# Moving the router's logits of the last two token tiles out of TensorE's tail, with their sums made ahead

## The chip, the cores and the metric

The kernel runs on one core of one Trainium2 chip. The metric is the device time of one execution in microseconds (us); the kernel before has a median of 738.65 over three runs. A core has five engines that run side by side, each with its own queue of instructions: TensorE (PE, matrix products), VectorE (DVE), ScalarE (ACT), GpSimd (POOL) and SyncE (SP, which here issues nearly all transfers). An engine takes its instructions in the order of its queue; one that waits holds up all that stand behind it.

## What is computed

The reference has three stages. Retention attention (2 x 8 heads, 768 positions, head width 64, blocks of 64) gives x of 1536 tokens x 512. A dense mixture of four experts follows, weighted by each token's domain probabilities, and then a mixture of eight experts of which each token takes the one with the greatest logit:

```python
# first mixture, dense
p = domain_probs / (domain_probs.sum(-1, keepdims=True) + 1e-09)
for e in range(4):
    h = np.maximum(x @ w1[e], 0.0)            # 512 -> 1024
    out += p[:, e:e + 1] * (h @ w2[e])        # 1024 -> 512
# second mixture, x is now the first one's output
logits = x @ w_gate                           # 512 -> 8
expert_idx = np.argmax(logits, axis=1)
...
for e in range(8):                            # only the tokens of expert e
    h = np.maximum(x[mask] @ w1[e], 0.0)
    out[mask] = gate_w[mask, None] * (h @ w2[e])
```

All is float32. TensorE takes float32r here, so each operand is split into a high and a low part and each product is three (high x high, high x low, low x high); `mm3` at L595 is that product.

## The kernel before

The 1536 tokens are 12 tiles of 128. After the attention the first mixture runs in 16 units k = 0 to 15, each of them half an expert (512 hidden features) for half of the tokens (six tiles): k = 0 to 7 do the first half, 8 to 15 the second. Units 1 to 13 are fast units (`fast_unit`): the first products (L740, tiles named b) are made by seven products of half-size blocks instead of eight, written into PSUM banks, copied by ScalarE (L747, tiles u), summed by VectorE (`total`, L754, also on tiles u) and split into ht_..h and ht_..l (L602, L603); then six second products y (L595), each added into acc by VectorE (L636). The seven products share a few PSUM banks: the last product of a unit goes into two banks that `total` has read just before. In units 1 to 6 VectorE also makes the next units' first weights in the combined forms that the products need (L182, L251) and SP stores them in DRAM (kept, L247) for the second half. Work that isn't the products' own is hung on hooks: `hook1(i)`, i = 0 to 13, stands behind the 14 half products of a fast unit, and `hook2(j)`, j = 0 to 5, behind its second products.

The sum of the blocks that a fast unit needs comes from `x_sum` (L703), which for the second half's tokens runs in units 2 to 5, one call each at i = 1. x2 holds the second half's attention output, 128 x 4 x 768 float32, from the attention on until unit 7 makes its splits; from then on its place serves as a ring of five pieces of 512 columns in which rows of the router's weights lie, one row on all partitions.

The router's logits of six tiles are sums by VectorE, `logit_v` (L846): the product of a tile of acc (128 x 512) with one router row, reduced to one column of lg_v; 48 of them run in units 8 to 12. Units 14 and 15 run together as three blocks of 256 tokens (768, 1024, 1280, named by the first token), with plain products h and y; each block's steps are also hung on hooks, numbered through all the blocks. The choice of a tile (`route_choose`: maximum mx, score sc, m_all, one-hot oh, df, seen; L889 to L907) and its rank (`route_rank`, products with a triangle and with ones, L918, L920) are placed by `route_at` at such hooks.

The last block's two tiles are y (tile 10) and z (tile 11). y's second products are plain; z's are made in two halves of 256 columns (`last_dense`, tile yz, added to acc at L658). Their logits come from TensorE: acc is transposed (`route_x`, tile rtr, L858), copied, and multiplied with the router's weights (`route_lg`, tile lg, L869). Then come choice, rank, the selection (`first_sel`, sel), and the products that place the two tiles' rows among those of the second mixture's first expert (`first_place`, L1037, into px, where the rows that were gathered from DRAM have been transposed by `first_T`, L1006). VectorE and ScalarE split px into xg (L1418, L1419), and the first expert's products g (L1479, L1480) begin.

At the start, 54 matmuls on ones (`warmup`, L1098) run before the first scores; SP loads the attention's data meanwhile.

Of the kernel before, what the change touches and what calls it, by code (L numbers as in the profile page):

```python
# [77 lines left out]
def body(ctx: ExitStack, tc: tile.TileContext, lam, att, dp, w1a, w2a, wg, wgt, w1b, w2b, out):  # L78
# [29 lines left out]
    lg_v = const.tile([P, VT, E2], F32, name="lg_v")  # L108
# [33 lines left out]
    wt = {}  # L142
    raws = [rawp]
# [40 lines left out]
    def split_plain(n, c, only=""):  # L184
        b = blocks[n]
        k = b[1]
        if c == 0 and only != "l":
            wt[b] = tuple(
                wp.tile([P, 4, HF], F32R, tag=f"w{b[0]}{x}", name=f"w{b[0]}{x}_{b[1]}")
                for x in "hl"  # L190
            )
        if b in EARLY_AT and c < EARLY:
# [24 lines left out]

    kept = {
# [234 lines left out]
    def att_a(c):  # L453
# [7 lines left out]
        for r in range(2):  # L461
            V.tensor_tensor(out=a[r], in0=qk[r], in1=w[:, r], op=ALU.mult)
# [179 lines left out]
    def last_parts(hs, j, c, i):  # L642
        return [
            ((hh[:, j * P:j * P + P], hl[:, j * P:j * P + P]),
             tuple(w[:, f % FC, c] for w in wt[1, KL - 1 + f // FC]))
# [3 lines left out]
    def last_dense(hs, t0, j, m, i):  # L649
        t = t0 // P + j  # L650
        c = slice(m * HD, m * HD + HD)
        if i == 0:
            rt["yz"] = ps_mm.tile([P, 512], F32, tag="mm", name=f"yz{m}")[:, :HD]
        ps = rt["yz"]
# [133 lines left out]
    def open_routing():  # L788
        op = ctx.enter_context(pool("order", 1, side="right"))
        for name, n, d in (  # L790
            ("places", EN, F32), ("caps", EN, F32), ("count", E2, F32), ("place", EN, F32),
            ("cap_e", E2, F32), ("nth", EN, I32), ("tmp", E2 * max(OMAX, E2), F32),
# [41 lines left out]

    def logit_piece(e):
        i = e % RING * DM
        return x2.rearrange("p d t -> p (d t)")[:, i:i + DM]
# [7 lines left out]
    def logit_v(t, e):  # L845
# [4 lines left out]
        if t == TT - 1:  # L850
            logit_load(e + RING)

# [22 lines left out]
    def route_choose(t):  # L875
        rp = rt["rs"]
        if t < VT:
# [79 lines left out]

    def last_sends():
        rp = rt["rs"]
        n = 2  # L960
        two = slice(NC - n, NC)
        sums, far, at_row = (
            rp.tile([P, n], F32, name=f"two{i}", bufs=1) for i in range(3)
        )
        pos = rp.tile([P, n], I32, name="twopos", bufs=1)
        for i in range(n):
            t = NC - n + i
            oh, _, df, _ = rt.pop((t, "chosen"))
            ex = rp.tile([P, E2], F32, tag="ex", name=f"ex{t}")
            A.activation(out=ex, in_=df, func=AF.Exp, accum_out=sums[:, i:i + 1])  # L970
            jk = rp.tile([P, E2], F32, tag="jk", name=f"jk{t}")
# [5 lines left out]
            out=at_row, in0=m2_all[:, two], scalar1=-float(MOST), scalar2=float(E2 * MOST),  # L977
            op0=ALU.mult, op1=ALU.add,
        )
        V.tensor_scalar(  # L980
# [3 lines left out]
        V.tensor_tensor(out=at_row, in0=at_row, in1=far, op=ALU.add)  # L984
        V.tensor_tensor(out=pos, in0=at_row, in1=rk_all[:, two], op=ALU.add)
        V.tensor_scalar(out=sums, in0=sums, scalar1=1e-9, scalar2=None, op0=ALU.add)
        V.reciprocal(acc[:, two, DM], sums)
        for i in range(n):
            t = NC - n + i
            scatter(bins, pos[:, i:i + 1], acc[:, t, :], E2 * MOST, "bins")  # L990
# [10 lines left out]
    def first_T(s):  # L1001
        if s == 0:
            px = [ps_mm.tile([P, 512], F32, tag="mm", name=f"px{d}") for d in range(2)]
            rt["px"] = [px[d // 2][:, d % 2 * CAP:d % 2 * CAP + CAP] for d in range(KD)]
        for d in range(KD):
            T.matmul(  # L1006
                rt["px"][d][:, s * ST:s * ST + ST], rt["xe"][:ST, s, d * P:d * P + P],
                ident[:ST, :ST], start=s == 0 and d % 2 == 0, stop=False, is_transpose=True,
# [34 lines left out]
    def route_order():  # L1043
        count, place, places = od["count"], od["place"], od["places"]
        by_pair = od["tmp"][:, :EN * EN].rearrange("p (a b) -> p a b", a=EN)
        sm = rt["warm"][:, :E2]
# [53 lines left out]
    def keep_up(n):  # L1100
        rt["warm"] = small("warm_rt")
        warmup(rt["warm"], n)


    with tc.manual_schedule():
# [13 lines left out]
        warmup(warm, 54)  # L1119
# [166 lines left out]
        for i, now in enumerate((  # L1286
# [7 lines left out]
            if now[-1] in ((b, 7), (c, 2)):  # L1294
                for d in range(E2 - RING):
                    at(8 + i, logit_load, d if now[-1] == (b, 7) else RING + d)
        route_at(a, 17, 18)
# [7 lines left out]
        for k in FAST:  # L1305
            def logit(n):
                for _ in range(n):
                    if logits:
                        logit_v(*logits.pop(0))
# [12 lines left out]

            def hook2(j):
# [10 lines left out]
                if k in KEPT:  # L1334
                    logit(2 if k == KS else 2 - j % 2)
# [5 lines left out]
            if k == KS - 1:  # L1341
                for e in range(RING):
                    logit_load(e)
                logits = [(t, e) for e in range(E2) for t in range(TT)]
# [5 lines left out]
        for t0 in range(TS, N, 256):  # L1350
# [16 lines left out]
            if last:  # L1367
                split_to(0, K1 + 1, 4)
                state["owed"] = 0
                split_to(1, K1, EARLY)  # L1370
                first_load()
            for j in range(256 // P - last):
                moe1_mm2(KL, hs, t0, j)
                if not last:
                    unit(2 * FC + j)
        assert not plan
        y, z = NC - 2, NC - 1
        low, high = range(KD // 2), range(KD // 2, KD)
        first_parts(y)
        last_dense(hs, t0, 1, 0, 0)  # L1380
        route_x(y)
        last_dense(hs, t0, 1, 0, 1)
        last_dense(hs, t0, 1, 1, 0)
        first_parts(z, slice(0, HD))
        route_x(z, low)
        last_dense(hs, t0, 1, 1, 1)
        route_lg(y)
# [478 lines left out]
```

## Time and profile before

| what | us |
|---|---|
| median of three runs | 738.65 |
| lowest and highest of them | 738.19, 739.57 |
| the profiled execution, its own time | 739.93 |
| its span in the trace | 738.1 |
| attention and unit 0 | 0 to 78.67 |
| fast units 1 to 13, 31.55 each but for the first and the last | 78.67 to 489.88 |
| units 14 and 15 in blocks of 256 tokens | 489.88 to 554.4 |
| last tiles' routing | 554.4 to 568.8 |
| second mixture | 568.8 to 729.84 |
| last sums and stores | to 738.1 |

One profiled execution is read: when each instruction began and how long it took, what it waited for, and what the transfers did. The span is the stretch from its first to its last instruction; 1.8 us of the execution's own time lie around it. The stages are read off the chain of waits, the chain of work that ended last, followed back from the last instruction.

### The profile page before, as it was taken

The page shows a single profiled execution, that of the slowest core. Times are in us where ns is not written, and L with a number is a line of the kernel's source. Part 1 is how long each engine was busy: PE and PEld are TensorE (multiplying, and loading weights), DVE is VectorE, ACT ScalarE, POOL GpSimd, SP SyncE. Part 2 cuts the span into 40 slices and gives each one's busy share as a digit, 9 for nine tenths or more (in the row PEclk, how much of TensorE's full clock was granted, in tenths as well). Part 3 has the DMA queues.
Part 4 walks back from the last instruction along what each step waited for, and adds up shares of the span by engine and source line. Part 5 has one row for each costly group of instructions (what it writes and reads, how often), then busy time and mean ns, then how long its engine had stood idle before and what let it go on. Part 6 is the DMA issues. An engine that isn't in the chain of part 4 may idle for free.

```text
span 738.1 us, 12981 instructions
## 1 busy us (share of the span) xinstructions
PE 727.1 (99%) x4951; PEld 658.9 (89%) x4951; DVE 510.9 (69%) x1140; ACT 313.7 (42%) x690; POOL 81.2 (11%) x86
## 2 busy tenths in 40 slices
PE   9999999999999999999999999999999999999995
PEld 8888989889898988989889898988898998998994
DVE  7557776776756766657677667774696867675883
ACT  4333725243342535424223141541153757565772
POOL 3474000000000000000000002100021013121013
PEclk9999999999999999999999999999999999999998
DMA  8763794626446175455161543361143968765661
GB/s 315 286 217 104 249 262 175 256 93 255 158 180 256 58 284 229 155 202 212 59 257 38 218 156 145 100 200 39 52 113 133 323 222 270 255 209 187 229 231 32
DMA packets 39420, 136.79 MB, mean 185 GB/s; under 512 B 6913, under 2 KB 6913, under 8 KB 34747
## 3 DMA queue, kind: packets, MB, share of 16 engines
q1 hardware_dynamic: 37243, 129.63, 50.6%
q0 software_dynamic: 2112, 6.31, 2.2%
q8 instruction: 40, 0.66, 0.4%
q14 instruction: 25, 0.20, 0.1%
HBM read 102.85 MB, written 33.26 MB: 184 GB/s over the span
## 4 chain that ended last, share of the span: by engine, by line
PE 96%; DVE 1%; ACT 1%; issue 1%; POOL 0%; POOLq 0%; DVEq 0%
PE y L595 36%; PE b L740 26%; PE h L595 7%; PE g L595 5%; PE z L595 3%; PE z L1479 3%; PE g L1479 2%; PE zr L1588 2%; PE qk L395 1%; PE z L1480 1%; PE g L1480 1%; PE xo L529 1%; PE zr L1559 1%; PE warm L1098 1%; PE yz L595 1%; PE gr L595 1%
## 5 line engine op out<-in xcount | busy, mean ns | idle before, releaser
L210 DVE TENSOR_TENSOR w1l<-raw,w1h 128x512 fp32r<-128x512 f32 x124 | 82.4, 688 | 28.5 <-ACT w1h L208 28.1
L636 DVE SCALAR_TENSOR_TENSOR acc<-y,p_sb,acc 128x512 f32<-128x512 f32 x77 | 57.8, 751 | 61.2 <-PE y L595 54.2
L747 ACT COPY u<-b 128x384 f32<-128x384 f32 x78 | 36.4, 479 | 108.6 <-PE b L740 107.1
L208 ACT CAST w1h<-raw 128x512 fp32r<-128x512 f32 x124 | 73.1, 619 | 1.1 <-DMA raw<-in_w2a 1.1
L125 POOL DMA_INDIRECT bins<-acc,pos x10 | 11.2, 1117 | 456.9 <-DVE mx L889 378.5
L740 PE MATMUL b<-xh,w0h 128*128 128x384 f32 x208 | 57.8, 339 | 0.0
L210 DVE TENSOR_TENSOR w0l<-raw,w0h 128x512 fp32r<-128x512 f32 x76 | 51.2, 722 | 0.8 <-ACT w0h L208 0.6
L846 DVE CUSTOM_DVE_ANT_0 x<-acc,x 128x512 f32<-128x512 f32 x72 | 49.4, 687 | 1.0
L208 ACT CAST w0h<-raw 128x512 fp32r<-128x512 f32 x76 | 42.9, 623 | 4.5 <-DMA raw<-in_w1a 4.0
L125 POOL DMA_INDIRECT out<-y,xb x16 | 30.0, 1878 | 132.6 <-DVE y L1625 82.8
L754 DVE TENSOR_TENSOR u<-b,u 128x384 f32<-128x384 f32 x78 | 43.1, 552 | 1.4 <-PE b L740 1.4
L740 PEld LDWEIGHTS b<-xh,w0h 128*128 128x128 f32 x208 | 38.2, 188 | 0.6
L595 PE MATMUL g<-xg,w0h 128*128 128x288 f32 (+1 forms) x192 | 38.1, 294 | 0.0
L595 PE MATMUL h<-xh,w0h 128*128 128x256 f32 x144 | 36.0, 292 | 0.2 <-ACT xh L181 0.2
L740 PE MATMUL b<-xl,w0h 128*128 128x384 f32 x104 | 35.2, 339 | 0.0
L595 PE MATMUL h<-xh,w0l 128*128 128x256 f32 x144 | 34.7, 282 | 0.1
L740 PE MATMUL b<-t1h,w0h 128*128 128x384 f32 x104 | 30.8, 337 | 0.0
L595 PEld LDWEIGHTS g<-xg,w0h 128*128 128x128 f32 x192 | 30.8, 188 | 0.0
L740 PE MATMUL b<-xh,w0l 128*128 128x384 f32 x104 | 28.8, 338 | 0.0
L740 PE MATMUL b<-t4h,w0l 128*128 128x384 f32 x104 | 28.8, 337 | 0.0
L740 PE MATMUL b<-t2h,w0l 128*128 128x384 f32 x104 | 28.7, 337 | 0.0
L740 PE MATMUL b<-t3h,w0h 128*128 128x384 f32 x104 | 28.6, 336 | 0.0
(371 smaller groups left out, 2053.6 us busy)
## 6 DMA issues: line engine op xcount, KB each, us to landing
raw<-in_w2a SPq DMA_DIRECT2D x32, 512.0 KB, 3.5
raw<-in_w1b SPq DMA_DIRECT2D x32, 512.0 KB, 5.7
raw<-in_w2b SPq DMA_DIRECT2D x32, 512.0 KB, 4.4
kept<-w0h SPq DMA_DIRECT2D x12, 1024.0 KB, 7.9
w0h<-kept SPq DMA_DIRECT2D x12, 1024.0 KB, 9.5
raw<-in_w1a SPq DMA_DIRECT2D x18, 512.0 KB, 3.7
att<-in_att SPq DMA_DIRECT2D x12, 512.0 KB, 4.7
kept<-w0l SPq DMA_DIRECT2D x6, 1024.0 KB, 6.6
```

The source lines that it names most:

```text
L125: i = G.indirect_dma_start(out=dst, out_offset=bass.IndirectOffsetOnAxis(ap=idx, axis=0), in_=src, in_offset=None, bounds_check=rows - 1, ...
L208: A.copy(out=hi, in_=t)
L210: V.tensor_tensor(out=lo, in0=t, in1=hi.bitcast(F32), op=ALU.subtract)
L595: T.matmul(ps, l, r, start=first and i == 0, stop=last and i == len(ops) - 1)
L636: V.scalar_tensor_tensor(out=acc[:, t, 0:DM], in0=ps, scalar=p_sb[:, t, e:e + 1], in1=acc[:, t, 0:DM], op0=ALU.mult, op1=ALU.add,)
L740: T.matmul(ps, l[:, d, c], r[:, d, :], start=first and i == 0, stop=i == len(ops) - 1, skip_group_check=not first,)
L747: A.copy(out=t, in_=bank[2, s])
L754: V.tensor_tensor(out=t, in0=bank[b, s], in1=t, op=ALU.add)
L846: V.tensor_tensor_reduce(out=x2.rearrange("p d t -> p (d t)")[:, RING * DM:], in0=acc[:, t, 0:DM], in1=logit_piece(e), scale=1.0, scalar=0 ...
L1479: T.matmul(ps[:, :2 * n], wh, both, start=i == 0, stop=False)
L1480: T.matmul(ps[:, :n], wl, hi, start=False, stop=i == len(parts) - 1)
L1588: T.matmul(ps[s][:st], l[:, c], r, start=h == 0 and j == 0, stop=h == 1 and j == len(ops) - 1)
```

## The change

For the last two tiles the logits no longer come from transposes and products with the router. A logit of a tile is the sum of what the tile has in acc so far, times a router column, and of what the last expert half still adds; the latter is h times (w2 times the router column). So:

- Before the end, VectorE makes the two tiles' logits from their sums so far: 16 more `logit_v`, hung on hooks 1, 3, 5, 6 and 7 of the blocks, where hook 7 has six, and on hooks 15, 16 and 17.
- The second weights of the last expert get eight more columns, w2 times w_gate: the weight tiles of w2 are 520 columns wide, and the right halves of the two tiles' last products are 264 wide. Their last eight columns are added to lg_v, times the expert's probability (`lg_v<-yz`, 128 x 8).
- The eight columns for the last expert's eight row blocks are 64 sums of 512 products over a piece of w2 (`wg_v`, a VectorE product with reduction as in `logit_v`). 40 are hung on units 2 to 6, eight each (hook1 at i = 5, 9, 13 and hook2 at j = 0 to 4), and 24 on units 8 to 12 between the 48 logits. Each piece of w2 (128 x 512, 256 KB) is a load of its own, as is each router row.
- For the first 40, router rows and pieces of w2 lie in x2's place. So x2 is stored to DRAM at the end of unit 1 (`parked<-x`) and read back in unit 7; the four `x_sum` calls of the second half move from units 2 to 5 to unit 1 (i = 3, 5, 9, 11).
- The tail is written in another order: y's right half first, its choice, its left half, z's right half in two parts, z's left half, with the ranks between them; the transposes into px come behind, one bank for each of the four blocks d, in the order 2, 3, 0, 1; part of the places of the last two tiles goes to GpSimd.
- The warm-up has 46 matmuls instead of 54, and the first two attention tiles' product with the decay is made in halves. The loads of two raw pieces and the gathered rows change places at the start of the second mixture.

The diff, cut:

```diff
     def last_dense(hs, t0, j, m, i):
         t = t0 // P + j
-        c = slice(m * HD, m * HD + HD)
+        c = slice(m * HD, m * HD + HD + m * E2)
...
-        if i == 1:
+        if i == 1 and m:
             e = half(KL) // 2
             V.scalar_tensor_tensor(
-                out=acc[:, t, c], in0=ps, scalar=p_sb[:, t, e:e + 1], in1=acc[:, t, c],
-                op0=ALU.mult, op1=ALU.add,
-            )
+                out=lg_v[:, t, :], in0=ps[:, HD:], scalar=p_sb[:, t, e:e + 1],
+                in1=lg_v[:, t, :], op0=ALU.mult, op1=ALU.add,
+            )
...
+    def wg_v(u, e):
+        i = (u % (2 * FC)) * E2 + e
+        V.tensor_tensor_reduce(
+            out=x2_piece(RING), in0=od["wg", u],
+            in1=logit_piece(e) if u >= WG_PIECES - 2 * FC else x2_piece(e % 3), scale=1.0,
+            scalar=0.0, op0=ALU.mult, op1=ALU.add, accum_out=od["lw"][:, i:i + 1],
+        )
...
+        for hook, *now in (
+            (1, (y, 3)), (3, (z, 3)), (5, (y, 4)), (6, (z, 4)),
+            (7, (y, 5), (z, 5), (y, 6), (z, 6), (y, 7), (z, 7)),
+            (15, (y, 0)), (16, (z, 0)), (17, (y, 1), (z, 1), (y, 2), (z, 2)),
+        ):
+            for x in now:
+                at(hook, logit_v, *x)
+        at(12, wg_columns)
...
-                elif KS < k < K1 - 4:
-                    logit(i < 6)
-                elif i == 1 and 1 < k < 6:
-                    x_sum((3, 1, 2, 4)[k - 2], 1)
+                elif 1 < k < KS - 1:
+                    logit(i in (5, 9, 13))
+                elif k in KEPT:
+                    logit(i in (3, 7, 9, 13) and (i > 3 or k > KS))
...
+                if k == 1 and i in (3, 5, 9, 11):
+                    x_sum({3: 3, 5: 1, 9: 2, 11: 4}[i], 1)
+                if k == KS - 1 and i == 0:
+                    SP.dma_start(out=x2, in_=parked)
...
+            if k == 1:
+                SP.dma_start(out=parked, in_=x2)
+                for e in WG_PASSES[0]:
+                    wg_row(e)
+                wg_load(0)
+                wg_load(1)
+                logits = wg_steps(0) + wg_steps(1)
...
-        warmup(warm, 54)
+        warmup(warm, 46)
```

Where the instructions stand. SP, from the last stores of unit 1 to the first loads of unit 2 (kept is the store of the combined weights, raw a piece of weights, x the place of x2), before:

```order
L247 DMA kept_88<-w0h_2_1664 128x2048
L247 DMA kept_88<-w0l_3_1684 128x1024
L167 DMA raw_1753<-in_w2a 128x1024
L167 DMA raw_1794<-in_w2a 128x1024
L247 DMA kept_89<-w0h_0_1889 128x2048
```

and now:

```order
L251 DMA kept_89<-w0h_2_1666 128x2048
L251 DMA kept_89<-w0l_3_1686 128x1024
L1427 DMA parked<-x_103 128x3072
L885 DMA x_103<-in_wgt 128x512 x3
L881 DMA x_103<-in_w2a 128x512 x2
L168 DMA raw_1760<-in_w2a 128x1024
L168 DMA raw_1802<-in_w2a 128x1024
```

Six transfers stand between the last kept store and the next raw pieces; the five loads write the place that the store of x2 reads.

VectorE, in the first products of unit 2 (w1l is the low part of a second weight, u the total of a product, ht its split), before:

```order
L754 TENSOR_TENSOR u_2_1736<-b_2_1773,u_2_1736 128x384
L603 SCALAR_TENSOR_TENSOR ht_001l<-u_2_1736,ht_001h 128x384
L210 TENSOR_TENSOR w1l_1726<-raw_1522,w1h_1725 128x512
L754 TENSOR_TENSOR u_2_1802<-b_2_1785,u_2_1802 128x384
L603 SCALAR_TENSOR_TENSOR ht_110l<-u_2_1802,ht_110h 128x384
```

and now (the rows with lw are a sum and the reading of its result):

```order
L769 TENSOR_TENSOR u_2_1744<-b_2_1780,u_2_1744 128x384
L610 SCALAR_TENSOR_TENSOR ht_001l<-u_2_1744,ht_001h 128x384
L889 ISA x_103,lw<-x_103 128x512
L889 ISA lw 128x1
L213 TENSOR_TENSOR w1l_1734<-raw_1522,w1h_1733 128x512
L769 TENSOR_TENSOR u_2_1810<-b_2_1793,u_2_1810 128x384
L610 SCALAR_TENSOR_TENSOR ht_110l<-u_2_1810,ht_110h 128x384
```

The first sum stands between two splits and ahead of the total u that frees a bank for the last product of the unit.

VectorE in the tail, from the weight splits to y's choice (yz are the last products, lg the logits), before:

```order
L1021 TENSOR_TENSOR al_5877<-acc,ah_5876 128x512
L658 SCALAR_TENSOR_TENSOR acc<-yz_5880,p_sb,acc 128x256
L1021 TENSOR_TENSOR al_5927<-acc,ah_5926 128x256
L658 SCALAR_TENSOR_TENSOR acc<-yz_5913,p_sb,acc 128x256
L889 TENSOR_REDUCE mx_5963<-lg_5948 128x1
L891 SCALAR_TENSOR_TENSOR sc_5965<-lg_5948,mx_5963,desc 128x8
```

and now:

```order
L213 TENSOR_TENSOR wel_1_5959<-raw_5864,weh_1_5958 128x512
L665 SCALAR_TENSOR_TENSOR lg_v<-yz_5971,p_sb,lg_v 128x8
L951 TENSOR_REDUCE mx_5997<-lg_v 128x1
L953 SCALAR_TENSOR_TENSOR sc_5999<-lg_v,mx_5997,desc 128x8
L956 TENSOR_REDUCE m_all<-sc_5999 128x1
L957 TENSOR_SCALAR oh_6001<-sc_5999,m_all 128x8
L963 TENSOR_SCALAR df_5998<-lg_v,mx_5997 128x8
```

y's choice stood behind the sums and low parts of both tiles, and stands now right behind the last weight split.

## Rows read from the trace of the kernel before

**Rows 1.** The page, parts 1 and 4: busy us and share; the chain's shares

```profile
PE 727.1 (99%) x4951; PEld 658.9 (89%) x4951; DVE 510.9 (69%) x1140; ACT 313.7 (42%) x690; POOL 81.2 (11%) x86
...
PE 96%; DVE 1%; ACT 1%; issue 1%; POOL 0%; POOLq 0%; DVEq 0%
```

**Rows 2.** The chain of waits: start us, us, what

```profile
0.99 5.75 PE warm L1098 x54
6.73 1.99 PE qk L395 x32
...
554.42 1.43 PE yz L595 x12
...
568.39 0.43 PE g L1479
```

**Rows 3.** Timeline of SP: start us, us, engine line op out<-in xcount

```profile
1.17 0.89 SPq L340 DMA_DIRECT2D att<-in_att  x2
```

**Rows 4.** Transfers by kind, KB each, median us from issue to landing

```profile
att<-in_att SPq DMA_DIRECT2D x12, 512.0 KB, 4.7
...
x<-in_wgt SPq DMA_DIRECT2D x14, 256.0 KB, 3.2
```

**Rows 5.** Timeline of VectorE in unit 2

```profile
113.21 0.95 DVE L703 TENSOR_TENSOR acc<-x 128x768 f32<-128x768 f32 x1
...
119.89 0.55 DVE L754 TENSOR_TENSOR u<-b,u 128x384 f32<-128x384 f32 x1
...
121.51 0.55 DVE L754 TENSOR_TENSOR u<-b,u 128x384 f32<-128x384 f32 x1
```

**Rows 6.** Windows, units 1, 2: PE, PEld, DVE, ACT, POOL; clock, DMA, GB/s

```profile
78.67:110.42 31.75, 31.75 (x158) 28.16 (x157) 24.34 (x40) 14.80 (x30) 0.53 (x1) 1.00 0.96 293
110.42:141.97 31.55, 31.55 (x157) 28.24 (x157) 21.96 (x36) 12.62 (x25) 0.00 (x0) 1.00 0.56 210
```

**Rows 7.** Timeline of SP: kept stores of units 1, 2; five loads

```profile
106.81 0.33 SPq L247 DMA_DIRECT2D kept<-w0l  x1
...
138.36 0.44 SPq L247 DMA_DIRECT2D kept<-w0l  x1
...
301.38 2.23 SPq L841 DMA_DIRECT2D x<-in_wgt  x5
```

**Rows 8.** Windows, the same columns, behind unit 2's last kept store

```profile
138.00:140.00 2.00, 2.00 (x10) 1.58 (x10) 1.09 (x2) 0.00 (x0) 0.00 (x0) 1.00 1.02 420
...
145.50:146.00 0.50, 0.50 (x4) 0.50 (x4) 0.50 (x2) 0.00 (x0) 0.00 (x0) 1.00 0.19 74
```

**Rows 9.** The page, part 5: the logits' group, busy us, mean ns, idle before

```profile
L846 DVE CUSTOM_DVE_ANT_0 x<-acc,x 128x512 f32<-128x512 f32 x72 | 49.4, 687 | 1.0
```

**Rows 10.** Timeline of TensorE: unit 2's last product, and tile a's rank

```profile
122.82 0.34 PE L740 MATMUL b<-xh,w0l 128*128 128x384 f32 x1
...
529.62 0.18 PE L918 MATMUL rank<-oh,upper 128*128 128x8 bf16 x1
```

**Rows 11.** Windows, the same columns, after the last matmul

```profile
732.50:733.00 0.50, 0.00 (x0) 0.00 (x0) 0.00 (x0) 0.00 (x0) 0.00 (x0) 1.00 0.50 172
...
733.50:734.00 0.50, 0.00 (x0) 0.00 (x0) 0.00 (x0) 0.00 (x0) 0.00 (x0) 0.50 0.00 0
```

**Rows 12.** Timeline of VectorE: tile a's choice, and the tail

```profile
525.57 0.15 DVE L889 TENSOR_REDUCE mx<-lg_v 128x1 f32<-128x8 f32 x1
...
552.95 1.29 DVE L210 TENSOR_TENSOR wel<-raw,weh 128x512 fp32r<-128x512 f32 x2
...
558.70 0.43 DVE L1021 TENSOR_TENSOR al<-acc,ah 128x256 fp32r<-128x256 f32 x1 [0.47 <-ACT ah L1019]
...
561.65 0.17 DVE L889 TENSOR_REDUCE mx<-lg 128x1 f32<-128x8 f32 x1 [0.38 <-PE lg L869]
...
562.31 0.23 DVE L895 TENSOR_SCALAR oh<-sc,m_all 128x8 bf16<-128x8 f32 x1
```

More of the change, by code (lines that the diff above doesn't have):

```diff
@@ L851, in logit_v, with wg_load, wg_row, wg_steps @@
             logit_load(e + RING)
+    WG_PASSES = ((0, 1, 2), (3, 4), (5, 6, 7))
+    WG_PIECES = len(WG_PASSES) * 2 * FC
+    def wg_load(u):
+        if u >= WG_PIECES - 2 * FC:
+            t = st["sf"].tile([P, 2, HF // 2], F32, tag="sf", name=f"wg{u}")
+            t = t.rearrange("p a b -> p (a b)")
+        else:
+            t = x2_piece(3 + u % 2)
+        f = u % (2 * FC)
+        k = half(KL - 1 + f // FC)
+        SP.dma_start(out=t, in_=w2a[k // 2, k % 2, :, f % FC, :])
+        od["wg", u] = t
+    def wg_row(e):
+        SP.dma_start(out=x2_piece(e % 3), in_=wgt[e:e + 1, :].to_broadcast([P, DM]))
+    def wg_v(u, e):
[5 more added lines that the diff above has]
+        )
+    def wg_steps(n):
+        steps = []
+        last = n == len(WG_PASSES) - 1
+        for f in range(2 * FC):
+            u = n * 2 * FC + f
+            for e in WG_PASSES[n]:
+                steps.append([(wg_v, u, e)])
+            ahead = u + (3 if last else 2)
+            if ahead < (WG_PIECES if last else WG_PIECES - 2 * FC):
+                steps[-1].append((wg_load, ahead))
+        if not last and n + 1 < len(WG_PASSES) - 1:
+            steps[-1] += [(wg_row, e) for e in WG_PASSES[n + 1]]
+        return steps
+    def wg_columns():
+        lw = od["lw"].rearrange("p (f e) -> p f e", e=E2)
+        for i in range(2):
+            hi, lo = (t[:, :, HF:] for t in wx[1, KL - 1 + i])
+            hi_lo(hi, lo, lw[:, i * FC:i * FC + FC, :])
     def route_x(t, ds=range(KD)):
@@ L983, in last_sends, with last_scatter @@
         )
[L984 to L990, printed above, removed]
+        V.tensor_tensor(out=at_row, in0=at_row, in1=rk_all[:, two], op=ALU.add)
+        V.tensor_scalar(out=gates, in0=gates, scalar1=1e-9, scalar2=None, op0=ALU.add)
+        V.tensor_tensor(out=pos, in0=at_row, in1=far, op=ALU.add)
+        V.reciprocal(acc[:, two, DM], gates)
+    def last_scatter(i):
+        scatter(bins, rt["pos"][:, i:i + 1], acc[:, NC - 2 + i, :], E2 * MOST, "bins")
     def first_load():
@@ L1307, in logit @@
                 for _ in range(n):
[L1308 to L1309 removed]
+                    for what, *args in logits.pop(0) if logits else ():
+                        what(*args)
             def hook1(i):
@@ L1367, in body @@
             if last:
+                state["owed"] = 0
                 split_to(0, K1 + 1, 4)
-                state["owed"] = 0
                 split_to(1, K1, EARLY)
                 first_load()
-            for j in range(256 // P - last):
+                while state["load"] < 2 * (loads.index((1, K1 + 1)) + 1):
+                    load_piece()
+                    state["owed"] -= 1
+                break
+            for j in range(256 // P):
                 moe1_mm2(KL, hs, t0, j)
-                if not last:
-                    unit(2 * FC + j)
+                unit(2 * FC + j)
@@ L1396, in body @@
-        first_sel(y)
-        route_choose(z)
+        rt["counts"] = small("counts")[:, :E2]
+        T.matmul(rt["counts"], ones, rt["seen"], start=True, stop=True)
         first_place(y, low)
-        route_rank(z)
-        first_place(y, high)
-        keep_up(1)
-        T.matmul(rt["warm"][:, :E2], ones, rt["seen"], start=True, stop=True)
-        first_sel(z)
-        first_parts(z, slice(HD, DM), "l")
-        first_place(z)
-        last_sends()
+        first_place(z, low)
         x_ctx.close()
```

170 lines of the change are left out of this document (107 added, 63 removed).

## The prediction, made before the changed kernel ran

> **What bounds the kernel now.** The page's first part gives TensorE 727.1 us of a span of 738.1, and in the chain of waits the reader should see that one engine: 96% of it is TensorE [rows 1]. In the fast units it runs without a break, a block of products (L740) and a block of second products (L595) in turn. So work that is taken from VectorE, ScalarE or a transfer gives nothing by itself, and work that is added there costs nothing, as long as TensorE never waits for it. What matters is where TensorE waits, and the change touches two such places: the start (warm-up, then the first scores), and the last two tiles' routing, where the chain goes from the last dense product (yz) over the router's choice to the first product of the second mixture [rows 2]. It may make a third, in unit 2. The profiled execution took 739.93 us, 1.3 above the median of the three runs, 738.65; terms are read from that execution and added to the median, since each is a few us long and 0.2% of it is nothing.
>
> **The start.** The 54 warm-up matmuls run for 5.75 us, 0.106 each, and the scores follow at once, at 6.73 [rows 2]. The first attention data is issued at 1.17 [rows 3], and that kind lands 4.7 us after its issue [rows 4], so at 5.9. Eight matmuls fewer are 8 x 0.106 = 0.85 us, which would put the scores at 5.88, just where the data lands: the gain is at most 0.85. VectorE's first product is halved for two tiles; each half starts an instruction more, but ScalarE and TensorE can begin on the first half. I take -0.6, between -0.2 and -1.0.
>
> **The sums of units 2 to 6, and the store that goes ahead of them.** This is the dear part. The 40 sums write and read rows that lie in x2's place, so x2 (128 x 3072 f32, 1.57 MB) is stored at the end of unit 1, and the first loads into its place wait for that store. The order of SP shows the queue: the fourth kept store, the store of x2, three router rows, two pieces, and only then the next raw pieces. On VectorE the first sum stands ahead of a w1l and of the total u that ran at 119.89; the last product of unit 2 goes into the two banks that this u and the one at 121.51 read [rows 5]. If the sum waits, TensorE waits behind it.
>
> When could the first sum run? The four x_sums, 0.95 us in the row [rows 5] and 0.87 from one step to the next, now come into unit 1, where VectorE was busy 24.34 of 31.75 us [rows 6] but without a pause just where the kept pieces begin to be made. So these come up to 4 x 0.87 = 3.5 us later; a little is made up before the last one, and its store, issued at 106.81 [rows 7], goes at about 109.4. The same move makes TensorE wait some 0.45 us at the last product of unit 1. In unit 2 the same four stores were issued in the same rhythm, the last at 138.36 [rows 7]; the transfers then ran at 420 GB/s and had fallen to 74 by 145.5 to 146 [rows 8]: 7.1 us from the last issue to the end. So the queue comes free at 109.4 + 7.1 = 116.5. The store of x2 takes 1.57 MB / 0.42 = 3.7 us, until 120.2, and SP sees its landing up to 1 us later: 121.2. Five loads of the kind that follows took 2.23 us to issue, 0.45 each [rows 7], and land 3.2 us after their issue [rows 4]; the first piece is the fourth of them: 121.2 + 3 x 0.45 + 3.2 = 125.8, between 124.2 (no late notice, and the fourth kept store 0.6 earlier) and 127.7 (a second us of notice and as much more of queue).
>
> The sum takes 0.74 us (the like instruction of the logits is 0.69 [rows 9], and a read of 0.05 behind it), the w1l after it, of the same size, 0.6, the total u 0.55 [rows 5]: u is there at 127.7. TensorE came to the last product at 122.82 [rows 10], so it waits 4.4 us after its own 0.45, and as the second u comes 1.62 behind the first (119.89 to 121.51 [rows 5]) where half of that product takes 1.05, 0.6 more. Together 5.5 us, between 3.5 and 7.5. Nothing hides it: that VectorE loses an x_sum at the head of unit 2 is no help, the wait is for a transfer. Behind it VectorE has room (21.96 of 31.55 us in unit 2 [rows 6]; eight sums of 0.74 less one x_sum make 27), so units 3 to 6 cost 0 as long as the pieces are two ahead, and units 8 to 12, which hold as many sums a unit beside the logits, the same; if that room fails, some tenths each. The read-back of x2 in unit 7 has a block of products before its use: 0.
>
> **The clock behind that gap.** After the last matmul of the trace, which ends at 729.84, the granted clock is still 1.00 in the half microsecond from 732.5 and 0.50 in the one from 733.5 [rows 11]. A gap of 4.4 us in unit 2 is longer than the idle time that stands before that fall, so the clock may go to the lower level (1.2 GHz) here too. What it takes to come back no row shows directly; the warm-up ran at 0.106 us for 128 columns, where twelve products of 256 columns take 1.43 in the tail, 0.06 for 128 [rows 2]: a half-speed stretch of 5.5 us or so. The same after the gap would cost 5.5 / 2 = 2.75. Ends 0 and 2.75; as no row shows a fall inside the work, I take the middle, 1.4.
>
> A rule stands against this change here: the Trainium skill, "TensorE: Matmul & The Clock Gate", section "HAM oscillation — how this bites in real kernels", says that where bursts of matmuls pause for a DMA the clock gate falls to half rate and the next burst starts cold. By that rule the fall is sure, and the sum would be up to 1.35 us higher, at the end of 2.75. That the clock falls when TensorE rests, the end of this trace agrees with; no row of before shows it in a pause of the work.
>
> **The choice of an earlier tile.** Six more logits, 0.74 each, come into the hooks ahead of the rank of tile a: its maximum was at 525.57 [rows 12] and the rank product at 529.62 [rows 10]. With the 0.65 from maximum to one-hot that is 3.4 us of cover for 4.4 us of work, less the pauses that VectorE has there: +0.35, between 0 and 0.8.
>
> **The tail.** TensorE loses eight transposes and sixteen products with the router, and gains eight columns in 48 products: 48 x 8 columns x 1.43 / (12 x 256) = 0.18 us [rows 2]. But what bounds the change there is VectorE: it splits weights until 554.24 (552.95 + 1.29 [rows 12]), and these still stand ahead of the first choice. From there, with a tile's choice from maximum to one-hot 0.89 us (561.65 to 562.31 + 0.23 [rows 12]), y's one-hot is there at 555.4 with its sum of logits before it. Then two halves of y, each a sum of some 0.5, a wait of 0.47 for ScalarE's high part and a low part of 0.43 [rows 12], and a selection of some 0.4: 558.7. The sum and choice of z: 559.8, where TensorE, which has 60 products of 0.12 behind it since 548.8, has reached z's rank at 559.0 and waits 0.8. After that z's right sum, eight small steps (1 us) and z's two low parts, the last at 563.7; the last placing product ends at 564.0, its rows' splits take some 1 us, and the last piece of the first g starts at about 564.9 instead of 568.39 [rows 2]. That is -3.5, between -2.5 and -4.2. What comes behind (scatter, gathered rows, raw pieces) moves earlier by as much, so I let it stand to the end.
>
> **Sum.** -0.6 + 5.5 + 1.4 + 0.35 - 3.5 = +3.15; 738.65 + 3.15 = 741.8.
>
> **Rivals.** (1) *No wait in unit 2; faster.* If the first sum runs by about 121.5, u is there when TensorE comes, the 5.5 shrinks to 0.45 and there is no gap for the clock: -0.6 + 0.45 + 0.35 - 3.5 = -3.3, 735.4. For it: transfers fill just over half of unit 2 (DMA share 0.56 [rows 6]). Against it: they are full exactly where the store of x2 queues. It decides by some 4 us of landing. (2) *The wait, but the clock stays:* +1.75, 740.4. For it: the only fall in the trace comes after work that did not go on. (3) *About half the wait,* because the store overlaps the kept one or the pieces land sooner: 1 to 4 us in all, no fall, cancelled by the tail, 737.2 to 740.1. (4) *The tail gives nothing,* TensorE waiting for VectorE in place of its own products: 745.3 with the rest as forecast; the working above has every wait of VectorE in it and still ends 3.5 us earlier, so this gets little and lies in the first case's 0.40.
>
> **Chances.** The forecast (wait and fall) 0.40, the wait without a fall 0.18, half a wait 0.20, no wait 0.22. A measurement here tells 0.2%, 1.5 us, from no change, so "same" is 737.2 to 740.1. Slower: the forecast and half of the second, 0.50 with rounding; same: the third and half of the second, 0.28; faster: 0.22. The range goes from 736.0, which leaves out most of the no-wait case, to 744.5: the wait at 7.5, the clock at its full price or the tail at -2.5.
>
> **What would show it.** Right: TensorE idle for 4 to 5 us at 123 to 128, released by VectorE, which stands behind a piece's transfer itself; a granted clock of 0.50 after it; the last piece of the first g 3.5 us earlier, counted from the last block of y. Wrong: if unit 2 is as long as unit 3, there was no wait; if VectorE still places the last rows past 566, counted as before, the tail is mis-sized; if units 8 to 12 grow, the sums cost more than their room.

## The result

The changed kernel takes 744.55 us (median of six runs, 742.84 to 745.25), the kernel before 738.60 (six runs, 738.19 to 739.57): a ratio of 1.0074, with a 95% interval of 1.0063 to 1.0084. It is slower by about 5.9 us, where 3.15 was forecast; the median lies at the upper end of the range, 0.05 above it. The profiled execution took 744.28 us, its span is 742.5.

The page of the changed kernel, part 1 (busy time, share of the span, instructions), against [rows 1]:

```profile
PE 724.7 (98%) x4942; PEld 658.7 (89%) x4942; DVE 556.8 (75%) x1309; ACT 311.9 (42%) x690; POOL 81.5 (11%) x87
```

TensorE is busy 2.4 us less than before (its start and its tail lost work, and unit 2 took 3.0 us more, see below), VectorE is busy 46 us more for the sums, and the span is 4.4 longer: there must be idle time of TensorE that was not there. The waits of TensorE (what waited, for whom, total us, times, longest) name it:

```profile
PE b L755 <- DVE u L769: 6.0, 1, 6.0
PE qk L399 <- DMA att<-in_att: 1.1, 1, 1.1
PE warm L1164 <- POOL ones L1177: 1.0, 1, 1.0
PE rank L980 <- DVE oh L957: 0.8, 2, 0.7
```

One wait of 6.0 us for a total u, in one place. The windows of units 1, 2 and 3 (us; PE, PEld, DVE, ACT, POOL busy with their counts; granted clock, DMA share, GB/s), which answer to [rows 6], show where:

```profile
77.02:108.90 31.88, 31.88 (x157) 28.02 (x156) 27.58 (x45) 14.96 (x30) 0.53 (x1) 1.00 0.94 284
108.90:149.46 40.56, 34.52 (x158) 30.76 (x157) 25.64 (x51) 12.58 (x25) 0.00 (x0) 0.92 0.64 236
149.46:180.90 31.44, 31.44 (x157) 28.21 (x156) 25.04 (x50) 12.59 (x25) 0.00 (x0) 1.00 0.57 203
```

Unit 2 is 9.0 us longer than before, and its 40.56 us come apart in the row itself: TensorE is busy 34.52, so 6.0 are rest, and 34.52 is 3.0 more than 31.55 for the same products, at a mean clock of 0.92. Units 1 and 3, with the four x_sums and with eight sums, have their old length to within 0.2 us.

The way into the wait is read from three timelines (start us, us, engine, line, operation, count, and the idle time before it with its releaser). SP first, which answers to [rows 7]: the last kept store, the store of x2, and the loads that wait for it.

```profile
107.59 0.95 SPq L251 DMA_DIRECT2D kept<-w0l  x1
108.59 0.93 SPq L1427 DMA_DIRECT2D parked<-x  x1
120.20 1.28 SPq L885 DMA_DIRECT2D x<-in_wgt  x3
121.53 0.90 SPq L881 DMA_DIRECT2D x<-in_w2a  x2
```

The store is issued at 108.59 and only 11.6 us later may SP issue the first load. VectorE, against [rows 5]:

```profile
117.40 0.56 DVE L610 SCALAR_TENSOR_TENSOR ht_001l<-u,ht_001h 128x384 fp32r<-128x384 f32 x1 [0.59 <-ACT ht_001h L609]
126.13 0.69 DVE L889 CUSTOM_DVE_ANT_0 x<-x 128x512 f32<-128x512 f32 x1 [8.18 <-DMA x<-in_w2a]
...
127.35 0.55 DVE L769 TENSOR_TENSOR u<-b,u 128x384 f32<-128x384 f32 x1
```

VectorE stands still for 8.18 us at the first sum, and the total u behind it runs at 127.35, though its inputs were there long before. TensorE, against [rows 10]:

```profile
127.96 0.69 PE L755 MATMUL b<-xh,w0l 128*128 128x384 f32 x1 [6.04 <-DVE u L769]
128.44 0.52 PE L755 MATMUL b<-xl,w0l 128*128 128x384 f32 x1
128.76 0.52 PE L755 MATMUL b<-xh,w0l 128*128 128x384 f32 x1
```

A product of this shape takes 0.52 here where [rows 10] has 0.34. Matmuls overlap, so the distance of the starts tells the pace better: 0.32 us from 128.44 to 128.76, where the same two starts before lie 0.17 apart (123.00 and 123.17). The windows around it, in the columns of above:

```profile
126.00:126.50 0.50, 0.00 (x0) 0.00 (x0) 0.37 (x1) 0.00 (x0) 0.00 (x0) 1.00 1.09 442
126.50:127.00 0.50, 0.00 (x0) 0.00 (x0) 0.50 (x3) 0.00 (x0) 0.00 (x0) 0.79 0.88 360
127.00:127.50 0.50, 0.00 (x0) 0.00 (x0) 0.50 (x2) 0.00 (x0) 0.00 (x0) 0.50 0.41 164
...
133.00:133.50 0.50, 0.50 (x3) 0.40 (x2) 0.23 (x1) 0.24 (x1) 0.00 (x0) 0.50 0.16 33
133.50:134.00 0.50, 0.50 (x3) 0.37 (x3) 0.50 (x2) 0.00 (x0) 0.00 (x0) 0.88 0.00 0
```

The granted clock falls to 0.50, the level of 1.2 GHz, while TensorE rests, and stays there for the first 5.7 us of its work (127.96 to about 133.6), which therefore give half of what they take: 2.8 us lost.

The tail did what was forecast of it. TensorE waits once, 0.67 us for z's one-hot, and VectorE's last low part of z ends at 571.2. The last block of y begins at 556.64 here and at 548.65 before; counted from there, that low part ends at 563.2 (forecast 563.7), and the last piece of the first g, the second row, starts 3.8 us earlier than its row in [rows 2]:

```profile
567.75 0.17 PE L980 MATMUL rank<-oh,upper 128*128 128x8 bf16 x1 [0.67 <-DVE oh L957]
...
572.59 0.43 PE L1582 MATMUL g<-xg,w0h 128*128 128x352 f32 x1
```

The starts of the same steps in the traces show where each difference arises:

| step of TensorE (start, us) | before | changed | shift |
|---|---|---|---|
| first products of unit 1 | 78.51 | 77.02 | -1.5 |
| second products of unit 1 | 93.39 | 92.22 | -1.2 |
| second products of unit 2 | 124.93 | 131.96 | +7.0 |
| first products of unit 3 | 141.80 | 149.46 | +7.7 |
| units 14 and 15 | 489.72 | 497.55 | +7.8 |
| rank of tile a | 529.62 | 537.66 | +8.0 |
| second products of expert 0, third group | 584.33 | 588.80 | +4.5 |
| last products | 725.39 | 729.86 | +4.5 |

So unit 2 costs 8.8 us from its predecessor's second products on, the units behind it to 13 cost 0.2, the rank 0.2, and the tail gives back 3.6. The 1.5 us at the start are another matter: the profiled execution of the kernel before took 739.93, 1.3 above its median, and the experiments on the start below show no gain of that size in the medians.

### The profile page after: what moved, and what is told of

It reads as the page before. It is cut to its first block, busy times and chain, and to the rows that moved or that the text cites. A ratio compares the mean times of both kernels' runs of the same rounds, so it can differ in the third digit from the quotient of the medians.

```text
span 742.5 us, 13191 instructions
## 1 busy us (share of the span) xinstructions
PE 724.7 (98%) x4942; PEld 658.7 (89%) x4942; DVE 556.8 (75%) x1309; ACT 311.9 (42%) x690; POOL 81.5 (11%) x87
## 5 line engine op out<-in xcount | busy, mean ns | idle before, releaser
L863 DVE CUSTOM_DVE_ANT_0 x<-acc,x 128x512 f32<-128x512 f32 x88 | 60.5, 688 | 1.6
L755 PE MATMUL b<-xh,w0l 128*128 128x384 f32 x104 | 30.5, 355 | 6.0 <-DVE u L769 6.0
L889 DVE CUSTOM_DVE_ANT_0 x<-x 128x512 f32<-128x512 f32 x40 | 27.4, 684 | 9.1 <-DMA x<-in_w2a 8.2
```

The costliest lines, as they stand in the source:

```text
L755: T.matmul(ps, l[:, d, c], r[:, d, :], start=first and i == 0, stop=i == len(ops) - 1, skip_group_check=not first,)
L863: V.tensor_tensor_reduce(out=x2.rearrange("p d t -> p (d t)")[:, RING * DM:], in0=acc[:, t, 0:DM], in1=logit_piece(e), scale=1.0, scalar=0 ...
L889: V.tensor_tensor_reduce(out=x2_piece(RING), in0=od["wg", u], in1=logit_piece(e) if u >= WG_PIECES - 2 * FC else x2_piece(e % 3), scale=1. ...
```

## The experiments

**The sums of unit 2 moved behind its first products.**

```diff
-                    logit(i in (5, 9, 13))
+                    logit(k > 2 and i in (5, 9, 13))
...
-                    logit(j < 5)
+                    logit(j < 5 or 2 < k < KS - 2)
```

> The changed kernel, but in unit 2 no sum is hung on the hooks of the first products; its three go to units 3 to 5, one more each behind the second products. The store of x2, the loads and the number of sums stay. Theory (one wait: the first sum stands in VectorE's queue ahead of the total that frees a bank, for 8.2 us until its piece lands, TensorE idles 6.0 and then runs 5.7 us at the lower clock, 2.9 lost): the whole 8.9 goes, 744.55 - 8.9 = 735.7 (735 to 736.6), unit 2 is as long as unit 3, the clock is 1.00 all through. Rival (the 64 sums and their transfers cost by their amount, 46 us more of VectorE and 10.7 MB more of transfers): the wait comes back in units 2 to 6, 740 to 744.

Measured: 735.09 us (734.79 to 735.46), a ratio of 0.9950 [0.9937, 0.9962] to the kernel before. Run once more beside another kernel (below):

> The kernel with the three sums moved away, once more beside the one before it, so that the two are compared on one chip: 735.1, and its ratio to the kernel before 0.994 to 0.996.

It took 735.18 us, 0.9950 [0.9937, 0.9964]. The store still holds the loads up, to 120.84 us, but the first sum, now at 129.15, finds its piece there. The window of unit 2:

```profile
108.76:140.30 31.54, 31.54 (x157) 28.34 (x156) 24.01 (x45) 12.59 (x25) 0.00 (x0) 1.00 0.79 297
```

31.54 us and a clock of 1.00: the whole of the loss is gone, with all 64 sums and all their transfers in place. The theory of the one wait stands, the rival that the sums cost by their amount falls. This kernel is also faster than both.

**TensorE kept at work during the wait.**

```diff
+            if k == 2 and (p, s) == (3, 0):
+                warmup(ps_mm.tile([P, 512], F32, tag="mm", name="fill"), 90)
             product(p, s)
```

> The changed kernel with 90 matmuls of 128 columns on ones put in ahead of the last product of unit 2, which the idle time of 6.0 us has room for (90 x 0.06 = 5.4 us). Nothing that is computed hangs on them. Theory (the 2.9 us behind the wait are the clock, which falls because TensorE rests): wait as long as before, but granted clock 1.00 all through and the product block behind it at full pace: 744.55 - 2.9 = 741.6. Rival (the slow stretch has another cause, the transfers or VectorE's load at that time): no change, 744.5, clock 0.50 from about 126.5.

Measured: 741.25 us (median; 740.55 to 745.44), 1.0040 [1.0025, 1.0054]. The timeline of TensorE shows the rest filled and the products behind it at their old pace:

```profile
121.49 5.20 PE L1166 MATMUL fill<-ones 128*128 128x128 bf16 x90
126.50 0.44 PE L755 MATMUL b<-xh,w0l 128*128 128x384 f32 x1
126.79 0.34 PE L755 MATMUL b<-xl,w0l 128*128 128x384 f32 x1
...
128.12 0.45 PE L755 MATMUL b<-xh,w0l 128*128 128x384 f32 x1 [0.29 <-DVE u L769]
```

and its windows a clock of 1.00, with the same transfers under way:

```profile
121.50:126.50 5.00, 5.00 (x91) 5.00 (x90) 1.77 (x4) 0.01 (x1) 0.00 (x0) 1.00 0.88 322
126.50:129.00 2.50, 2.21 (x15) 1.89 (x13) 1.37 (x3) 1.41 (x4) 0.00 (x0) 1.00 0.60 218
```

Work that nobody needs made the kernel 3.3 us faster by the medians, though TensorE still had to wait for the same total. So the slow stretch is the clock's answer to the rest and not something that the transfers do. The three medians part the loss: 744.55 - 741.25 = 3.3 for the clock, 741.25 - 735.09 = 6.2 for the wait. The traces point the same way, but are not so clean: from unit 1's second products to unit 3 the changed kernel takes 8.8 us more than the kernel before, this one 5.7. The profiled execution is the fastest of the nine, and its first sum began at 124.68, so that TensorE had 5.0 us to fill and 0.3 to wait, not 6.0. One of the nine took 745.44, at a mean granted clock of 0.995 where the other eight have 0.996 to 0.998; the cause is open.

**The store of x2 ahead of the kept stores.**

```diff
+                if k == 1 and i == 11:
+                    SP.dma_start(out=parked, in_=x2)
...
             if k == 1:
-                SP.dma_start(out=parked, in_=x2)
```

> The changed kernel, but the store of x2 is issued in unit 1 right after the last x_sum, ahead of the four kept stores instead of behind them; the sums stay where they are, the first one ahead of the total. Theory (the piece is late because the store queues behind 4.5 MB of other transfers and the loads wait for it): the store lands by some 105, the loads are issued at 108 to 109 and have only the kept stores ahead of them, the first piece lands at 117 to 120 instead of 126.1; wait of TensorE 0 to 1.5, clock 1.00, 735.7 to 737.2. Rival (the load itself is slow, or the sums by their amount): wait stays over 3 us, over 741.

Measured: 739.05 us (median of twelve runs, 736.90 to 740.45), 1.0000 [0.9989, 1.0011]. This was missed by 2 us. SP no longer waits for the store, but issues slowly:

```profile
95.79 0.43 SPq L1393 DMA_DIRECT2D parked<-x  x1
...
107.94 2.72 SPq L885 DMA_DIRECT2D x<-in_wgt  x3
...
111.51 2.82 SPq L881 DMA_DIRECT2D x<-in_w2a  x2
```

The piece was there at 121.83, some 4 us earlier than in the changed kernel and 2 later than expected. It now has the kept stores themselves ahead of it, and the DMA share is 1.01 from 117 to 119; that these stores are what delays it fits, and was not tried. TensorE rests 2.07 us:

```profile
123.65 0.45 PE L755 MATMUL b<-xh,w0l 128*128 128x384 f32 x1 [2.07 <-DVE u L769]
...
125.27 0.69 PE L755 MATMUL b<-xh,w0l 128*128 128x384 f32 x1 [0.29 <-DVE u L769]
```

and even behind that the clock, expected to stay at 1.00, fell for a while:

```profile
121.60:123.60 2.00, 0.00 (x0) 0.00 (x0) 1.77 (x4) 0.00 (x0) 0.00 (x0) 1.00 0.20 80
123.60:125.00 1.40, 1.32 (x6) 1.01 (x6) 0.81 (x2) 0.52 (x1) 0.00 (x0) 0.98 0.61 214
125.00:127.50 2.50, 2.23 (x7) 2.23 (x8) 1.91 (x6) 1.28 (x3) 0.00 (x0) 0.50 0.23 90
```

The runs spread over 3.5 us: three near 737.0, one at 737.9, eight from 738.9 to 740.5. The mean granted clock of each execution parts them in the same way: 0.996 to 0.997 in the four faster ones, 0.994 to 0.995 in the eight others, the profiled one (739.12) at 0.994 among them. So the fall of the clock came in the eight and not in the four. The theory holds in the direction (an earlier piece, a shorter wait, a faster kernel), and its estimate of the landing was too low.

**The store made twice.**

```diff
                 SP.dma_start(out=parked, in_=x2)
+                SP.dma_start(out=parked, in_=x2)
```

> The changed kernel with x2 stored twice to the same place, one behind the other, so that the loads of the router rows wait for another 1.57 MB. Theory (the wait is the store's way through the queue, and the clock's price is paid once, however long the rest): the first piece lands 3.7 us later, TensorE idles 9.7 instead of 6.0, the slow stretch behind it stays 5 to 6 us: 744.55 + 3.7 = 748.3. Rival (a fixed time of the landing or of the loads sets the wait, or the clock's price grows with the rest): under 746, or over 750.

Measured: 748.54 us (four runs, 746.77 to 749.24), 1.0132 [1.0118, 1.0147]; 4.0 us more than the changed kernel, where 3.7 were expected. SP and the wait:

```profile
108.39 1.00 SPq L1427 DMA_DIRECT2D parked<-x  x1
119.16 0.32 SPq L1428 DMA_DIRECT2D parked<-x  x1
124.16 1.28 SPq L885 DMA_DIRECT2D x<-in_wgt  x3
```

```profile
PE b L755 <- DVE u L769: 10.1, 1, 10.1
```

The second store goes out only when the first has landed, and takes 5.0 us with no other store ahead of it; the rest of TensorE grows by 4.1, and the time by 4.0 in the medians (2.5 between the two profiled executions). Its clock is 0.50 again until about 135:

```profile
131.80:135.00 3.20, 3.16 (x10) 3.17 (x11) 2.04 (x4) 1.80 (x4) 0.00 (x0) 0.50 0.47 164
135.00:137.00 2.00, 2.00 (x11) 1.73 (x10) 1.56 (x5) 0.41 (x1) 0.00 (x0) 0.98 0.00 0
```

In this execution (746.77, the fastest of the four) 3.2 us of work run at the lower level, where 5 to 6 were expected, against 5.7 in the changed kernel's after a shorter rest. The mean granted clock goes down as the four get slower: 0.989, 0.988, 0.987 and 0.987. So the price of the fall does not grow with the rest; it differs from execution to execution.

**No sums at all.** This kernel leaves out the 64 sums, their loads and the store of x2, so that the last two tiles' logits lack the last expert half.

> The changed kernel without the 64 sums, their loads, and the store and read-back of x2; the eight columns are zero, so the last expert half's share in the last two tiles' logits is left out. The start, the moved x_sums, the 16 logits and the tail stay. Theory (outside the one wait the sums are hidden): 735.5, within 0.5 of the kernel with the sums moved out of the way. Rival (sums cost by their amount in the other units too): 1 to 3 us below that kernel.

Measured: 826.46 us, which answers the question only by its trace. With other logits some tokens go to other experts, more rows come to one than its place holds, and a loop for the rows left over runs behind the kernel; TensorE waits there:

```profile
PE o_tr L1883 <- DMA xo<-rest: 55.3, 2, 45.0
```

The main part is comparable. From the second products of unit 1 to the last products it takes 721.24 - 92.51 = 628.73 us, the kernel with the moved sums 720.63 - 91.99 = 628.64. So the 64 sums and their transfers cost nothing that shows outside the one wait.

**The start alone, on the kernel before:** 46 warm-up matmuls with the halves, and 46 without them.

```diff
-        warmup(warm, 54)
+        warmup(warm, 46)
```

> The kernel before with the changed start alone: 46 warm-up matmuls for 54, and the first two tiles' product with the decay in halves. Theory (as forecast, -0.6; the two traces show TensorE 0.9 us earlier from 19 us on): 737.9, between 737.6 and 738.4. Rival (the two traces differ at the start by chance, the scores wait for the data in place of the warm-up): no change, 738.5 to 738.7.

> The kernel before with 46 warm-up matmuls for 54 and nothing else. Theory (the gain of the start comes from the scores being earlier, at most 8 x 0.106 = 0.85): like the whole start, within 0.2. Rival (it comes from the halves): no change, 738.6, and the start as a whole is the faster one by half a us or more.

Measured: 738.30 us, 0.9995 [0.9987, 1.0004], and 738.36 us, 0.9998 [0.9990, 1.0007]. Neither can be told from no change. For the first this is the rival; the second lies within 0.2 of the first, as its theory said, but there is no gain for either to have. The trace of the first, too, stands 1.5 us ahead of the kernel before by unit 1 (77.02 against 78.51), with no gain in the median. What fits this is the spread of the kernel before: 17 of the 23 beside these two lie from 738.07 to 738.56 and six from 739.02 to 740.00, and the execution behind the rows, 739.93, is of the upper kind.

**The old start, with the moved sums:** 54 warm-up matmuls and no halves.

> The kernel with the three sums of unit 2 moved away, but with the old start: 54 warm-up matmuls and no halves. Theory (tail -3.5, rank +0.2, sums +0.2, so the start is what is left of -3.5 in all, 0 to -0.5): 735.1 to 735.6. Rival (the start is worth the 1.4 us by which the traces differ up to unit 1, and the sums cost a us somewhere): 736.2 or more.

Measured: 735.95 us (735.36 to 736.29), 0.9956 [0.9943, 0.9968], against 0.9950 with the new start: 0.4 us by the ratios, inside both intervals. The median lies between the two ranges written down (up to 735.6, and from 736.2). Taken from the medians, each less that of the kernel before beside it (738.32 here, 738.53 and 738.62 there), the start is worth 1.0 to 1.2. With the runs above, that makes it something between nothing and a microsecond; it is not settled.

**The weight splits of the tail behind the first rows.**

```diff
                 split_to(0, K1 + 1, 4)
-                split_to(1, K1, EARLY)
                 first_load()
...
         route_order()
+        split_to(1, K1, EARLY)
```

> The kernel with the three sums moved away, and in the tail the last two weight splits of 512 columns (weh, wel, 1.29 us of VectorE) written behind the split of the first expert's rows instead of ahead of y's choice. Theory (the tail's length is set by VectorE's queue, which is busy without a pause from the splits to the first expert's rows, and TensorE waits 0.7 us for z's one-hot): the choices come 1.2 us earlier, the wait for z's one-hot is gone, the first g starts 0.5 to 1.2 us earlier, 734.0 to 734.6. Rival (TensorE's own products set it): the first g no earlier than now, no change, 735.1, or slower if the late splits hold up the second products.

Measured: 735.35 us (735.10 to 736.04), 0.9954 [0.9941, 0.9968], beside 735.18 for the kernel without this edit: no change, as the rival had it, where 734.0 to 734.6 were expected. The mechanism was there and its gain was given back. The wait for z's one-hot, 0.67 in the kernel without the edit,

```profile
558.76 0.17 PE L980 MATMUL rank<-oh,upper 128*128 128x8 bf16 x1 [0.67 <-DVE oh L957]
```

shrinks to 0.2, and the first g starts 0.8 us earlier, counted from unit 1's first products. But the two splits now run at 565.22, ahead of VectorE's work for expert 0, whose last pair of splits before the second products begins at 570.59 instead of 569.49, though the first g began 0.1 us earlier in this trace. TensorE stands still at the second products of expert 0:

```profile
572.22 0.40 PE L1582 MATMUL z<-g,weh 128*128 128x352 f32 x1 [0.36 <-issue]
```

The row names no releaser; that it is VectorE's queue again fits the times and was not shown. Two steps on, the whole 0.8 us is gone. So VectorE's queue does set the tail's length up to the first g, as the sum had it, and what stands behind takes the gain back.

## Why the prediction was right, and where its sizes were off

The sign, the place and the chain of causes were as forecast; two terms were too small and one, the start, could not be shown.

| term | forecast | measured | from |
|---|---|---|---|
| the start | -0.6 | 0 to -1 | the start alone (ratio 0.9995); the old start with the moved sums |
| the wait in unit 2 | +5.5 | +6.2 | filled wait less moved sums, 741.25 - 735.09 |
| the clock behind it | +1.4 | +3.3 | changed less filled wait, 744.55 - 741.25 |
| the sums in other units | 0 | 0 to +0.2 | shift over units 3 to 13; the kernel without sums |
| tile a's rank | +0.35 | +0.2 | shift there |
| the tail | -3.5 | -3.6 | shift from tile a's rank to expert 0 |

**The wait.** The chain of its estimate can be held against the trace link by link. The forecast's times are on the scale of the rows, and the whole of the changed execution runs 1.2 us ahead of them by unit 1's second products (the table of starts), so 1.2 is added here to what was measured.

| link | forecast | measured + 1.2 |
|---|---|---|
| fourth kept store issued | 109.4 | 108.8 |
| first load allowed | 121.2 | 121.4 |
| first piece used | 125.8 | 127.3 |
| u ended | 127.7 | 129.1 |
| TensorE at the product | 123.3 | 123.1 |
| TensorE's rest | 4.4 | 6.04 |

TensorE's side came out, and the 1.6 us that are missing lie in the transfers. VectorE caught up 0.6 more of the moved x_sums than was assumed, but the way from the last kept store to the first load took 12.6 us instead of 11.8 (the section on the hardware shows its end), and the piece was used 5.9 us after that first load instead of 4.6; why the loads took longer was not tried. Unit 1's own wait came to 0.3 instead of 0.45 (the shift from -1.5 to -1.2). The 0.6 that the forecast added for the second u did not come on top, as the products ahead of it ran at half their pace; in the filled wait, at full pace, 0.29 of it shows. The first rival (no wait) asked for a first sum by 121.5 and missed it by 4.6 us.

**The clock** is the term that was mis-sized. The forecast took the middle of 0 and 2.75 for want of a row that showed a fall inside the work. The runs show 2.8 by the trace and 3.3 by the medians: its price of a fall was right to a tenth by the trace, and halving it was the miss. (It read that price from the pace of the warm-up, 0.106 us for 128 columns, against 90 such matmuls in 5.20 us in the filled wait; the profile gives the granted clock of that stretch as 1.00, so there the pace is the witness for the lower level and not the clock.) The second rival, a wait without a fall, would have given 740.4; the kernel with the filled wait is that rival made real, with 741.25. The rule of the Trainium skill, "TensorE: Matmul & The Clock Gate", "HAM oscillation — how this bites in real kernels", which speaks of bursts that start cold after a pause for a DMA, described what happened, and by it the sum would have been 743.15. The trace agrees with that rule: 0.50 from 127.0 to 133.5, and 1.00 where the pause was filled.

**The start** failed as a step, as far as the runs can tell. It took the 0.85 us that the warm-up ran over as a gain of the chain. The scores do begin earlier, at 6.17 instead of 6.66, though TensorE now waits 1.1 us for the data (the second row of the waits above). But what follows hangs on VectorE's weight splits, whose time varies from execution to execution (next section but one), and no gain is seen in the medians of the start alone. The term was also read in a trace that was 1.3 us slower than the median.

**The tail** came out to a tenth. The value of working it as VectorE's queue, operation by operation, shows in two numbers: z's one-hot makes TensorE wait 0.67 us (0.8 was worked out), and the shift is 3.6. One number in that working is wrong as it is written: 60 products of 0.12 us from 548.8 on would end at 556.0. Ahead of z's rank stand 84, and these give the 559.0 that the working goes on with; in the trace they end at 567.1, which is 559.1 on the scale of before.

## What to carry to other kernels

An instruction that waits for a transfer belongs behind everything in its engine's queue that others wait for; the same sums, with the first of them some 11 us later in VectorE's queue, made a change that cost 0.7% into one that gains 0.5%. A store that frees a place must be followed to its landing, through everything already queued, before the first load into that place can be dated. And the price of a rest of TensorE is not the rest alone: here it was half as much again for the clock, and dummy products in the gap, which are simple to place, took that half off.

## What the runs showed of the hardware that was not expected

A rest of 2.07 us was followed by a fall of the granted clock to 0.50 that came 1.3 us after TensorE had begun to work again, just as a second rest, of 0.29 us, began (the rows of the early store), so the level in a stretch need not match what the engine does in that stretch. How long the lower level then holds varied, 5.7 us of work in one kernel's execution and 3.2 in another's after a longer rest.

The landing of the store of x2 varied, too. The windows of the changed kernel, in the columns of above:

```profile
118.00:118.50 0.50, 0.50 (x5) 0.50 (x4) 0.00 (x0) 0.25 (x1) 0.00 (x0) 1.00 0.98 418
118.50:119.00 0.50, 0.50 (x5) 0.50 (x4) 0.00 (x0) 0.21 (x1) 0.00 (x0) 1.00 0.07 25
119.00:119.50 0.50, 0.50 (x5) 0.50 (x4) 0.00 (x0) 0.27 (x1) 0.00 (x0) 1.00 0.06 25
119.50:120.00 0.50, 0.50 (x5) 0.50 (x3) 0.00 (x0) 0.00 (x0) 0.00 (x0) 1.00 0.00 0
```

The transfers end at full rate by 118.5, then 25 GB/s trickle on for a microsecond, and SP issues its first load 0.7 us later still, at 120.20. In the kernel with the filled wait there is no trickle: the transfers stop by 118.5, and SP issues at 119.09. With the moved sums it lasts to 120.5, and SP issues at 120.84. From the issue of the store to the first load that makes 11.61, 10.78 and 12.45 us. The trace of before has a trickle, too, behind unit 2's kept stores (25 and 16 GB/s from 146 to 147). So the late notice of up to 1 us, for which the forecast had no row, is seen here; the trickle is not in its sum, and what causes it is open.

Two executions of the same start differ by 0.7 us at unit 1 (76.92 and 77.64), and the difference arises in VectorE's queue: four splits of 128 x 512 behind the attention took 4.22 us in one kernel and 5.32 in the other, in the timelines of VectorE of the kernel with the moved sums (second run) and of the one with the late tail splits:

```profile
11.45 4.22 DVE L213 TENSOR_TENSOR w0l<-raw,w0h 128x512 fp32r<-128x512 f32 x4
```

```profile
11.61 5.32 DVE L213 TENSOR_TENSOR w0l<-raw,w0h 128x512 fp32r<-128x512 f32 x4
```

The code of that stretch is the same in both. The same four splits took 5.31 us in the execution behind the rows of before and 4.22 in the changed kernel's, which, going by this pair, is about half of the 1.5 us between them at unit 1. Both traces with 54 warm-up matmuls show 5.31, and of the ten with 46 only one shows 5.32; whether the start sets this or chance does is not settled. What slows single splits there was not tried either. GpSimd works on products of its own in the same microseconds (12.04 to 16.82 and 12.07 to 16.38), which makes it a candidate. It stays open, and it is why a term of less than a microsecond at the start could not be read from one trace.
